# A planned attention and dense kernel: head, zero matmuls, last transposes, halved late values and a new order

## The chip, the cores and the metric

The kernel runs on one core of a Trainium2 chip. The metric is device time in microseconds, the median of a few runs. Beside the runs there is one profiled execution with a trace; all durations below are from it.

## What is computed

Two blocks, A and B, are applied twice, with the same weights both times.

```python
x = x + A(layernorm(x)); x = x + B(layernorm(x))
x = x + A(layernorm(x)); x = x + B(layernorm(x))

# A: 64 segments of 32 rows, one after the other
for s in range(64):
    h = concat([mem, xs])              # 8 memory rows + 32 rows = 40
    q, k, v = h @ Wq, h @ Wk, h @ Wv   # 512 -> 32 heads x 128
    p = softmax(where(mask, q @ k.T * scale, -1e9))
    o = (p @ v) @ Wo                   # 40 x 512
    mem, out[s] = o[:8], o[8:]
# B: relu(x @ w1) @ w2                 # 512 -> 1376 -> 512
```

There are 2048 rows in bf16. The memory makes A a recurrence: a segment can't start its projections before the output projection of the segment before it.

## The kernel before

**Two layers side by side.** The two applications of A run interleaved in 68 steps. Step k works on segment k of the first layer and segment k-4 of the second (`DELTA` = 4). In steps 4 to 63 both are active, and each matmul streams 80 columns, 40 of each layer; in steps 0 to 3 and 64 to 67 only one is, with 40 columns. The columns of a step lie transposed in one of two tiles HT, and the weights stay in SBUF.

**One step.** `step_values` multiplies HT's columns by Wv (L1006). `queries_keys` makes q and k in units of 4 heads, 16 matmuls each into a bank of `work`. `scores` does the score matmuls (L1090), then mask, maximum and subtraction on DVE (L1101, L1105, L1108), exp on ACT (L1112), sum and reciprocal on DVE (L1115, L1118), and the multiply that gives P on DVE or POOL (L1132). P is turned by a matmul with the identity, and ACT and DVE copy it to PT (L1155, L1157). `attend` multiplies PT by the values (L1174), and ACT copies the result to OT (L927, the line of the copy helper). `project` multiplies OT by Wo into the one bank `st`, in five parts, one per unit; "project.2" is the third of them. From `st` the eight new memory rows go to the next step's HT, and the rows go to OX. All matmuls that may run whole or in two 64-column tiles go through `across` and have line L671.

**After each odd step,** `finish_pair` takes 64 rows of each layer: a DMA transpose of OX on SP (L888), the residual add on DVE (L892), then `dense_layer` with its `layernorm` (statistics L712 and L715 on DVE, eps and power on POOL L718 and L719, norm on DVE L722, a DMA transpose on SP L736), w1 (L671), relu, w2 (L798 for 64 rows), an add (L813) and the store (L913). For the very last pair nothing is left to run beside this chain.

**The start.** `load_weights` issues the weights in the order Wv, Wq, Wk, Wo from SP (the first piece) and POOL. `prepare` loads the first 128 rows of x and the memory from ACT's queue, clears tiles on DVE and POOL, and clears the five `work` banks with copies from the zeroed V0 on ACT and DVE. The first rows are normalised (`prepare_group`), turned on PE, copied to a tile by ACT, and copied from there into HT by POOL in `prep_x` (L946). While weights land, PE makes the values of groups 1 to 7 of 128 rows ahead of time and stores them. The values of groups 8 to 15 are made later by `late_values`, eight ops of four 512-column matmuls for a pair of groups, put into the odd steps at certain step numbers (`SPREAD`); some odd steps so have two of them, some one, and from step 49 on none.

**The order.** Nothing is ordered by hand. `Plan` collects all ops with modelled costs and dependences, and `order` plays them through and emits one static order per engine. Which op goes next on PE is decided by a priority, `PERIOD * step + PLACE[op, phase]`; `phase` tells apart the first steps, even and odd steps and the last ones. For other engines the priority comes from the users of an op, less an entry of `AHEAD`. `RULE` holds four numbers: how far ahead a start may be looked for, how much staying in a tile mode is worth, and two for ops marked `spare`. `PAIRED` lists which projections (queries, keys, Wo) may run in two 64-column tiles ("64-column mode") rather than whole. An op with two engines takes the one on which it ends sooner by the model.

Of the kernel before, what the change touches and what calls it, by code (L numbers as in the profile page):

```python
# [9 lines left out]
F32 = mybir.dt.float32  # L10
# [20 lines left out]
RULE = (0.077, 191.201, 3554579.029, 1242705613.066)  # L31
PERIOD = 42.8582
PLACE = {
# [153 lines left out]
}  # L187

LOAD = {("v", 0): 4.4, ("v", 1): 3.8, "o": 2.95}
REST, SLOW = 2.75, 6.0  # L190

EARLY, SPREAD = 7, (0, 0, 2, 4, 4, 6, 8, 10)

# [225 lines left out]
def kernel(  # L419
# [185 lines left out]
    def prepare():  # L605

        def zero_columns():
            for t in HTs:
                nc.vector.memset(t[:], 0.0)
# [731 lines left out]
```

## Time and profile before

| quantity | value |
|---|---|
| median of 3 runs | 1618.84 us (1618.56 to 1620.61) |
| span of the profiled execution | 1619.3 us |
| instructions in it | 94084 |
| PE work per two steps in the middle | 47.1 us |
| last weights landed | 50.6 us |
| end of the last project | 1601.79 us |

The page of the profile gives the busy time of each engine, the span in 40 slices, the DMA queues, a chain of work that ended last, and the costliest groups of instructions. Here is what the slices look like for PE, and for the DMA engines:

```profile
PE   7899999999999999999999999999999999999996
...
DMA  9721111111111111111111111111111111111000
```

A digit is the busy share in tenths of a slice of 40 us. PE is nearly full from the second slice to the last but one, and the DMA engines only while the weights load. A row such as `L671 PE MATMUL st<-OT,Wo_sb` is a group: line, engine, operation, output, inputs.

### The profile page before, as it was taken

Reading aid. Unit: us, or ns where it says so; the run is one execution under the profiler, and the core shown is the slowest. Engines: PE = TensorE matmul, PEld = TensorE weight load, DVE = VectorE, ACT = ScalarE, POOL = GpSimd, SP = SyncE. Lnnn points to the kernel's source line nnn. Section 1 sums busy time; section 2 is a strip of 40 time slices with the busy share of each in tenths; the row PEclk is TensorE's granted clock in tenths of the full one; section 3 lists DMA queues with packets and bytes.
Section 4 is the critical chain, followed back from the end, with each engine's and each line's share of the span. In section 5 each row is a group of like instructions: output and inputs, shape, how many; then the busy total and the mean of one; then the engine's idle time right before and its main releaser. Section 6 shows DMA issues by size and latency. Waiting matters only on the chain.

```text
span 1619.3 us, 94084 instructions
## 1 busy us (share of the span) xinstructions
PE 1573.6 (97%) x42673; PEld 1355.0 (84%) x42673; DVE 1050.2 (65%) x2974; ACT 1058.4 (65%) x2672; POOL 160.7 (10%) x395
## 2 busy tenths in 40 slices
PE   7899999999999999999999999999999999999996
PEld 4678888888888888888888888888888888888875
DVE  4466666766766676676667667666766766676663
ACT  5567666766666676666667666666766666676663
POOL 4210000001100000110000011000000000000000
PEclk9999999999999999999999999999999999999998
DMA  9721111111111111111111111111111111111000
GB/s 374 244 50 35 30 29 36 33 34 40 36 31 30 36 33 34 40 33 33 31 36 33 34 40 33 34 31 36 33 34 30 30 28 27 27 27 27 21 15 11
DMA packets 88065, 74.03 MB, mean 46 GB/s; under 512 B 60584, under 2 KB 74000, under 8 KB 87664
## 3 DMA queue, kind: packets, MB, share of 16 engines
q1 hardware_dynamic: 81168, 46.64, 12.9%
q0 software_dynamic: 5328, 20.32, 3.3%
q8 instruction: 334, 5.47, 1.4%
q10 hardware_dynamic: 1168, 1.06, 0.2%
q14 instruction: 67, 0.55, 0.1%
HBM read 33.50 MB, written 11.93 MB: 28 GB/s over the span
## 4 chain that ended last, share of the span: by engine, by line
PE 95%; ACT 2%; DMA 1%; POOL 1%; issue 1%; DVE 1%; POOLq 0%; SPq 0%; DVEq 0%; ACTq 0%
PE work L671 40%; PE st L671 19%; PE fill L1006 16%; PE fill L671 11%; PE work L1174 4%; PE work L1090 3%; ACT OT L927 1%; DMA xr<-OX 0%; ACT HT L927 0%; PE fill L798 0%; DMA xnM<-xr 0%; DMA V<-vw 0%; ACT es L1112 0%; POOL ln L719 0%; ACT qT L927 0%
## 5 line engine op out<-in xcount | busy, mean ns | idle before, releaser
L671 PE MATMUL work<-HT,Wk_sb 128*128 128x80 bf16 (+2 forms) x9184 | 357.3, 199 | 11.5 <-ACT HT L927 9.3
L671 PE MATMUL work<-HT,Wq_sb 128*128 128x80 bf16 (+2 forms) x10624 | 357.6, 200 | 0.0
L671 PEld LDWEIGHTS <-Wk_sb 128*128 128x128 bf16 (+1 forms) x9184 | 326.3, 101 | 32.2 <-ACT HT L927 13.7
L671 PEld LDWEIGHTS <-Wq_sb 128*128 128x128 bf16 (+1 forms) x10624 | 328.4, 104 | 29.1 <-issue 16.2
L671 PE MATMUL st<-OT,Wo_sb 128*128 128x80 bf16 (+1 forms) x8704 | 334.7, 199 | 5.4 <-ACT OT L927 3.6
L671 PEld LDWEIGHTS <-Wo_sb 128*128 128x128 bf16 x8704 | 317.7, 99 | 15.4 <-issue 10.0
L1006 PE MATMUL fill<-Wv_sb,HT 128*64 128x512 bf16 x2176 | 281.8, 383 | 0.9 <-POOL HT L946 0.5
L927 ACT CAST kT<-work 128x320 bf16<-128x320 f32 (+1 forms) x517 | 211.8, 410 | 107.5 <-PE work L671 66.3
L927 ACT CAST qT<-work 128x320 bf16<-128x320 f32 (+1 forms) x505 | 207.7, 412 | 73.7 <-PE work L671 25.7
L1101 DVE TENSOR_TENSOR es<-work,maskb 128x320 f32<-128x320 f32 (+2 forms) x340 | 134.8, 405 | 127.6 <-PE work L1090 119.9
L927 ACT CAST OT<-work 128x320 bf16<-128x320 f32 (+1 forms) x351 | 132.6, 414 | 129.2 <-PE work L1174 128.6
L1155 ACT ACTIVATE PT<-work,half 128x320 bf16<-128x320 f32 (+1 forms) x406 | 181.8, 477 | 8.7 <-DVE PT L1157 4.0
L927 ACT CAST vw<-fill 128x512 bf16<-128x512 f32 x228 | 133.9, 587 | 76.3 <-PE fill L1006 73.4
L1006 PEld LDWEIGHTS <-HT 128*64 128x64 bf16 x2176 | 101.9, 110 | 62.7 <-issue 2.3
L1112 ACT ACTIVATE es<-es 128x320 f32<-128x320 f32 (+2 forms) x340 | 134.1, 405 | 18.3 <-DVE es L1108 14.4
L1108 DVE TENSOR_TENSOR es<-es,mx 128x320 f32<-128x320 f32 (+2 forms) x340 | 135.3, 406 | 4.5
L1157 DVE TENSOR_SCALAR PT<-work,half 128x160 bf16<-128x160 f32 (+2 forms) x274 | 116.2, 445 | 31.4 <-PE work L671 29.7
L1105 DVE TENSOR_REDUCE mx<-es 128x8 f32<-128x320 f32 (+2 forms) x340 | 132.6, 398 | 4.6
L1115 DVE TENSOR_REDUCE sm<-es 128x8 f32<-128x320 f32 (+2 forms) x340 | 129.7, 390 | 2.7 <-ACT es L1112 2.3
L1132 DVE TENSOR_TENSOR P<-es,sm 128x320 bf16<-128x320 f32 (+2 forms) x307 | 127.8, 426 | 5.4
L892 DVE TENSOR_TENSOR xg<-xg,xr 128x512 f32<-128x512 f32 (+1 forms) x34 | 23.5, 692 | 161.1 <-DMA xr<-OX 160.9
L1090 PEld LDWEIGHTS <-qT 128*40 128x40 bf16 x4096 | 87.4, 98 | 34.6 <-ACT qT L927 0.3
(91 smaller groups left out, 1701.1 us busy)
## 6 DMA issues: line engine op xcount, KB each, us to landing
V<-vw SPq DMA_DIRECT2D x240, 48.0 KB
V<-vh SPq DMA_DIRECT2D x120, 64.0 KB
Wq_sb<-in_A_Wq_dram POOLq DMA_DIRECT2D x2, 2048.0 KB, 20.3
Wk_sb<-in_A_Wk_dram POOLq DMA_DIRECT2D x2, 2048.0 KB, 24.8
Wo_sb<-in_A_Wo_dram POOLq DMA_DIRECT2D x2, 2048.0 KB, 36.4
vh<-vg SPq DMA_DIRECT2D x32, 128.0 KB
Wv_sb<-in_A_Wv_dram POOLq DMA_DIRECT2D x1, 2048.0 KB, 11.2
vh<-w_sb POOLq DMA_DIRECT2D x4, 512.0 KB, 7.7
```

The costliest lines, as they stand in the source:

```text
L671: nc.tensor.matmul(out_[u:v, :], lhsT=lhsT[:, u:v], rhs=rhs, start=start, stop=stop, tile_position=(0, u), **more)
L927: nc.scalar.copy(out=out_, in_=in_)
L1006: nc.tensor.matmul(vp[64 * b:64 * b + 64, :], lhsT=cols(c4), rhs=Wv_sb[:, c4, n * 512:(n + 1) * 512], start=(c4 == 0), stop=(c4 == NC4 - 1 ...
L1090: nc.tensor.matmul(v[64 * g2:64 * g2 + L, a, i, b, :], lhsT=qT[:, hi, a * L:(a + 1) * L], rhs=kT[:, hi, a * L:(a + 1) * L], start=True, st ...
L1101: nc.vector.tensor_tensor(out=flat(es[:, A]), in0=flat(sp[:, A]), op=ALU.add, in1=maskb[:, a_lo:a_hi, :].unsqueeze(2).to_broadcast([128, n ...
L1105: nc.vector.tensor_reduce(out=mx[:, As], in_=es3(), axis=AX.X, op=ALU.max)
L1108: nc.vector.tensor_tensor(out=es3(), in0=es3(), op=ALU.subtract, in1=mx[:, As].unsqueeze(2).to_broadcast([128, ns * na, L]))
L1112: nc.scalar.activation(out=es[:, A], in_=es[:, A], func=ACTF.Exp, scale=SCALE)
L1115: nc.vector.tensor_reduce(out=sm[:, As], in_=es3(), axis=AX.X, op=ALU.add)
L1132: (nc.gpsimd if eng == POOL else nc.vector).tensor_tensor(out=o, in0=flat(es[:, A]), op=ALU.mult, in1=sm[:, As].rearrange("p (a s) -> p a ...
L1155: nc.scalar.activation(out=o, in_=i, func=ACTF.Copy, scale=half[:, b:b + 1])
L1157: nc.vector.tensor_scalar_mul(out=o, in0=i, scalar1=half[:, b:b + 1])
```

## The change

It has six parts.

1. **First rows.** The load of x rows 0 to 127 moves from ACT's queue to SP, ahead of the first piece of Wv; in the plan that piece waits for the issue.
2. **Zero matmuls.** A new 128x256 tile `none` is zeroed by DVE. `spin` multiplies it by itself into a bank, two matmuls of 256 columns. Five of these clear the `work` banks in place of five copies from V0; eight more (`WARM`) only run. The first queries and keys wait for the clearing of their banks.
3. **A shorter first layernorm.** For the first rows and the last pair, eps is added on DVE, the power stays on POOL. For the first rows an added copy (`first`) puts the turned rows straight into HT, and `prep_x(0)` goes.
4. **The last pair** turns OX on PE (`turn_near`, four matmuls of 128 columns in a 64-column tile) instead of by DMA, followed by 20 zero matmuls (`idle(2.2)`). Its second transpose is on PE too, with a copy (`keep_near`).
5. **Late values** are planned as two ops of two matmuls in place of one of four.
6. **The order** is planned anew: all numbers in `RULE`, `PERIOD`, `PLACE`, `PAIRED` and `AHEAD` are others. The program has 44797 matmuls in place of 42673; 46 are zero matmuls, the rest come from ops that are now in 64-column mode (two matmuls for one). 270 queries and keys ops are in that mode, before 150. 28 more of the multiplies L1132 are on POOL.

The diff, its tables cut to a line each:

```diff
-RULE = (0.077, 191.201, 3554579.029, 1242705613.066)
-PERIOD = 42.8582
+RULE = (0.0787279, 46.129, 9.15314e+07, 211.005)
+PERIOD = 11.86222
...
+WARM = 8
...
-                    t, o = min((c for c in starts if c[0] <= due and c[0] + room * c[1].cost[e] * c[1].spare <= due), key=rank)
+                    t, o = min((c for c in starts if c[0] <= due and c[0] + room * c[1].cost[e] * c[1].spare <= due), key=rank,
+                               default=(t, o))
...
+    def get_x():
+        nc.sync.dma_start(out=xb0[:, :], in_=A_x[0, 0:128, :])
+
     def load_weights():
 
+        plan.op(SP, 0.78, get_x, w=[xb0, "x0"], lag=0.0)
...
+        def zero_none():
+            nc.vector.memset(none[:], 0.0)
...
-        def get_x():
-            nc.scalar.dma_start(out=xb0[:, :], in_=A_x[0, 0:128, :])
...
-            def zero_bank(eng, t=t):
-                copy_on(eng, t[:], V0[:].rearrange("p q n -> p (q n)").bitcast(F32)[:, 0:512])
+            def zero_bank(t=t):
+                spin(t)
...
+    def spin(bank):
+
+        for u in range(2):
+            nc.tensor.matmul(bank[:, 256 * u:256 * u + 256], lhsT=none[:, 0:128], rhs=none[:, :], start=True, stop=True)
+
+    def idle(t, r=()):
+        bank, n = b_fill.buf(), max(1, int(t / 0.218))
+
+        def spins():
+            for _ in range(n):
+                spin(bank)
+
+        plan.op(PE, t, spins, r=["none", *r], w=[bank], count=2 * n)
...
+        early, quick = not isinstance(xnT, Buf), near or xnT is first_rows
...
         def power():
-            nc.gpsimd.tensor_scalar_add(out=ln[R, 7:8], in0=ln[R, 7:8], scalar1=LN_EPS)
+            (nc.vector if quick else nc.gpsimd).tensor_scalar_add(out=ln[R, 7:8], in0=ln[R, 7:8], scalar1=LN_EPS)
+            if not quick:
+                raise_()
+
+        def raise_():
             nc.gpsimd.tensor_tensor(out=ln[R, 7:8], in0=ln[R, 7:8], in1=mhalf[R, :], op=ALU.pow)
...
+        if near:
+            plan.op(PE, 0.01 + 1.72e-3 * n, turn, r=[xn, "ident"], w=[tp], tile=EITHER, count=4)
+            copy_op(NC4 * n, keep_near, r=[tp], w=[xnT])
+            return xnT
...
+        if xnT is first_rows:
+            copy_op(NC4 * SEG, first, r=[tp], w=htx(0, 0))
...
+        last = j == NP + D2 - 1
+        if last:
+            y = b_fill.buf()
+
+        def turn_near():
+            for c4 in range(NC4):
+                nc.tensor.matmul(y[PR:2 * PR, 128 * c4:128 * c4 + 128], lhsT=ox[:, c4, PR:2 * PR], rhs=ident[:, :],
+                                 start=True, stop=True, tile_position=(0, PR))
...
-        plan.op(SP, XBAR[0] + XBAR[1] * NC4, turn, r=[ox], w=[y], lag=XBAR[2])
+        if last:
+            plan.op(PE, 0.22, turn_near, r=[ox, "ident"], w=[y, "turned"], tile=COL64, count=NC4)
+            idle(2.2, ["turned"])
+        else:
+            plan.op(SP, XBAR[0] + XBAR[1] * NC4, turn, r=[ox], w=[y], lag=XBAR[2])
...
-        plan.op(PE, 0.2165 * NC4, mm, r=[*on(pair[0]), *on(pair[1]), *gate], w=[vp], tile=EITHER, spare=True,
-                count=NC4)
+        for c0 in range(0, NC4, 2):
+            def mm(cols, c0=c0):
+                for c4 in (c0, c0 + 1):
...
+            plan.op(PE, 0.433, mm, r=[*on(pair[0]), *on(pair[1]), *gate], w=[vp], tile=EITHER, spare=True, count=2)
...
-    plan.mark(0, "s")
-    prep_x(0)
```

More of the change, by code (lines that the diff above doesn't have):

```diff
@@ new lines @@
+    ("*layernorm.aggr", 1): 54551538274992652288, ("*layernorm.first", 1): -15140200627925014,
+    ("*layernorm.keep", 1): -349948822785553596416, ("*layernorm.norm", 1): -15140200627913234,
+    ("*layernorm.power", 1): 350004080033075429376, ("*layernorm.raise_", 1): 262488285178343948288,
+    ("*layernorm.stats", 1): -906.966, ("*prepare_group.load", 1): -54520433886651039744,
+    ("*values.ev", 1): 10798138046876852224, ("attend.ev", 0): -6284291257622319104, ("attend.ev", 1): 1079.491,
@@ new lines @@
+    ("attend.ev", 2): -2553479593618.246, ("bulk.land", 1): -238860144121.9,
+    ("dense_layer.relu", 0): -14914902342738771968, ("dense_layer.relu", 1): 10.441,
+    ("dense_layer.relu", 2): -135955653579501.906, ("dense_layer.relu_last", 0): 8630611085116452864,
+    ("dense_layer.relu_last", 1): 94558522.384, ("dense_layer.relu_last", 2): -135955653582153.484,
+    ("early_stores.put", 1): -2338178960349301760, ("finish_pair.add", 0): -754598561880401024,
+    ("finish_pair.add", 1): -541211854841342208, ("finish_pair.add", 2): -5135522821684.899,
@@ new lines @@
+    ("finish_pair.add0", 0): -8449851934466816, ("finish_pair.add0", 1): -2116007360007716096,
+    ("finish_pair.add1", 0): 678562308116700160, ("finish_pair.add1", 2): 517137148556446.5,
+    ("finish_pair.store", 0): -2736302177266691072, ("finish_pair.store", 2): -554122428120319,
+    ("finish_pair.turn", 0): 771228859628232576, ("finish_pair.turn", 1): -8411911657729126400,
+    ("finish_pair.turn", 2): 855769499775299712, ("finish_pair.widen", 0): -3434171858064559616,
+    ("finish_pair.widen", 1): -11285277819407153152, ("get_x", 1): -10804293557987115008,
@@ new lines @@
+    ("late_values.ev", 0): -338731664576501841920, ("late_values.put", 0): 124.155,
+    ("layernorm.aggr", 0): -338774959185562828800, ("layernorm.aggr", 1): -1283017268359357952,
+    ("layernorm.aggr", 2): -2124137526600.683, ("layernorm.keep", 0): -86307786047708640,
+    ("layernorm.keep_near", 2): -1932750949110.553, ("layernorm.norm", 0): -8180445813364675,
+    ("layernorm.norm", 1): 1256955092211969.5, ("layernorm.norm", 2): -587212723712585.5,
+    ("layernorm.power", 0): -3425991412251194880, ("layernorm.power", 1): 8667933725116555264,
@@ new lines @@
+    ("layernorm.power", 2): -179841382886347776, ("layernorm.raise_", 2): 180391610330498048,
+    ("layernorm.stats", 0): -513018287628265216, ("layernorm.stats", 1): -558147728977931648,
+    ("layernorm.stats", 2): -620728644676.763, ("layernorm.turn_far", 0): 1118984946535674880,
+    ("layernorm.turn_far", 1): 2119073176186372864, ("layernorm.turn_far", 2): -513925009903168.938,
+    ("load_dense.dma1", 1): -2518505793790285312, ("load_dense.dma2", 1): -537535825433483264,
+    ("load_group.get", 0): 1068285834928873088, ("load_group.get", 1): -352507446103958159360,
@@ new lines @@
+    ("load_group.load", 0): 674877631977439232, ("load_group.load", 1): 309263599505791320064,
+    ("load_weights.dma", 1): 174994470155083907072, ("make_ident", 1): 524983410226391613440,
+    ("make_mask", 1): 487564700809337831424, ("place_values.dma", 0): -2736302177266692608,
+    ("place_values.dma", 1): -6024653512617976, ("prep_x.cp", 0): -2948860633222666752,
+    ("prep_x.cp", 1): 349988940071307706368, ("prep_x.cp", 2): 179804397606783520,
+    ("prepare.get_memory", 1): 9013136272599680, ("prepare.keep", 1): 271359371850913447936,
@@ new lines @@
+    ("prepare.make_half", 1): 10785635464923846656, ("prepare.place", 1): -14327787264.792,
+    ("prepare.zero", 1): 111823167.023, ("prepare.zero_columns.zero", 1): -10793200354345601024,
+    ("prepare.zero_none", 1): 111823008.502, ("prepare.zero_ox", 1): 251674778347272568832,
+    ("prepare_group.load", 0): -503980667476090368, ("prepare_group.put", 0): -392362853562742272,
+    ("prepare_group.put", 1): -2338178004908725248, ("project.ev", 0): -109848075148066832,
+    ("project.ev", 1): -341038992002229338112, ("project.ev", 2): -1035549021077084.875,
@@ new lines @@
+    ("project.first", 1): -161879.785, ("project.rows", 0): -342058079058195644416,
+    ("project.rows", 1): -10204126385068992, ("project.rows", 2): 516497770743318.875,
+    ("queries_keys.ev", 0): -2688.654, ("queries_keys.ev", 1): 3379306714640166,
+    ("queries_keys.ev", 2): -1932750948659.773, ("scores.block", 0): -13588549336362629120,
+    ("scores.block", 1): 3.988, ("scores.block", 2): 1288500730644.738, ("scores.exp", 0): 13647408900884832256,
+    ("scores.exp", 1): -18932611.033, ("scores.exp", 2): -630011255086.4,
@@ new lines @@
+    ("scores.keep", 0): -340848835228960686080, ("scores.keep", 1): 3379306714647110.5,
+    ("scores.keep", 2): -1932750948086.011, ("scores.mul", 0): 179804397606588544,
+    ("scores.mul", 1): 2468249049887821.5, ("scores.mul", 2): 50246.546, ("scores.recip", 0): -14.277,
+    ("scores.recip", 1): 1068.112, ("scores.recip", 2): -1288500730305.69, ("scores.sub", 0): -13647408900884832256,
+    ("scores.sub", 1): 18932637.161, ("scores.sub", 2): -658489475543.995, ("scores.top", 0): -8271002289903067136,
@@ L187 @@
+    ("scores.top", 1): -70.887, ("scores.top", 2): -1923468696638.604, ("scores.total", 0): 8271002289903065088,
+    ("scores.total", 1): -48.963, ("scores.total", 2): 1288500731007.345, ("values.ev", 0): -2690.806,
+    ("values.ev", 1): 3379306714642456, ("values.ev", 2): -1932750949652.126,
 }
@@ L512, in dma @@
                     q.dma_start(out=W_s[c][:, :, cs], in_=W_v[c][:, :, cs])
-            bulk(POOL if (c, p0) != ("v", 0) else SP, 0.78, dma, (c, p0), n, w=[("W", c, p0 + i) for i in range(n)],
+            bulk(POOL if (c, p0) != ("v", 0) else SP, 0.78, dma, (c, p0), n, w=[("W", c, p0 + i) for i in range(n)], r=["x0"] if (c, p0) == ("v", 0) else [],
                  rate=LOAD.get((c, p0), LOAD.get(c, REST)))
@@ L588 @@
     V0 = sb("V0", [128, 4, 512])
+    none = sb("none", [128, 256])
     OT = sb("OT", [128, H, 2 * L])
@@ L605, in prepare, with zero_columns, zero @@
     def prepare():
-        def zero_columns():
-            for t in HTs:
-                nc.vector.memset(t[:], 0.0)
+        def zero_none():
+            nc.vector.memset(none[:], 0.0)
+        def zero_columns(i):
+            def zero():
+                nc.vector.memset(HTs[i][:], 0.0)
+            plan.op(DVE, 0.2, zero, w=[("HTm", i), *[("HTx", i, a, c) for a, c in ((0, 0), (1, X1))]])
         def make_half():
@@ L635, in place @@
             nc.vector.tensor_copy(out=HTs[0][:, :, MO[0]:MO[0] + M], in_=mem0T[:])
-        columns = [("HTm", i) for i in range(2)] + [("HTx", i, a, c) for i in range(2) for a, c in ((0, 0), (1, X1))]
-        plan.op(ACT, 0.45, get_x, w=[xb0, "x0"])
-        plan.op(ACT, 0.45, get_memory, r=["x0"], w=[mb0, "start"])
-        plan.available("memory", 7.5)
-        plan.op(DVE, 0.4, zero_columns, w=columns)
+        plan.op(ACT, 0.45, get_memory, w=[mb0, "start"])
+        plan.available("memory", 5.5)
+        plan.op(DVE, 0.13, zero_none, w=["none"])
+        for i in range(2):
+            zero_columns(i)
         plan.op(DVE, 0.25, make_half, w=["half"])
@@ L656, in prepare @@
         for i, t in enumerate(b_work.tiles):
-            def zero_bank(eng, t=t):
-                copy_on(eng, t[:], V0[:].rearrange("p q n -> p (q n)").bitcast(F32)[:, 0:512])
-            copy_op(512, zero_bank, r=[("V0", 0, 0)], w=[("bank", i)])
-        plan.op(POOL, 0.6, make_ident, r=[("issued", "v", 1)], w=["ident"])
+            def zero_bank(t=t):
+                spin(t)
+            plan.op(PE, 0.43, zero_bank, r=["none"], w=[("bank", i)], count=2)
+        for i in range(WARM):
+            idle(0.43 if i < 3 else 0.22, [("bank", j) for j in range(5)])
+        plan.op(POOL, 0.6, make_ident, w=["ident"])
         plan.op(POOL, 2.3, make_mask, w=["mask"])
@@ L694 @@
     hold, stores = [None], []
+    first_rows = p_xn[0].buf()
     def on(t):
@@ L702, in halves_of, with layernorm @@
         return t[:, :, :].rearrange("p q (h t) -> p q h t", h=2)
-    def layernorm(x, rows, xnT, lo=0, n=128, to=None, halved=False):
-        ln, xn, tp = p_ln.buf(), p_xr.buf(), b_fill.buf() if halved else None
+    def layernorm(x, rows, xnT, lo=0, n=128, to=None, halved=False, near=False):
+        ln, xn, tp = p_ln.buf(), p_xr.buf(), b_fill.buf() if halved or near else None
         R = slice(lo, lo + n)
         to = lo if to is None else to
-        early = not isinstance(xnT, Buf)
+        early, quick = not isinstance(xnT, Buf), near or xnT is first_rows
         def stats():
@@ L733, in keep, with keep_near, first @@
                     i.rearrange("p (q c h s) -> p q c h s", q=NC4, h=2, s=HS))
+        def keep_near(eng):
+            copy_on(eng, xnT[:, :, to:to + n], tp[:, 0:NC4 * n].rearrange("p (c t) -> p c t", c=NC4))
+        def first(eng):
+            copy_on(eng, HTs[0][:, :, 0:SEG].rearrange("p q (h s) -> p q h s", h=2),
+                    tp[:, 0:NC4 * n].rearrange("p (q h c s) -> p q h c s", q=NC4, h=2, s=HS)[:, :, :, 0, :])
         def turn_far():
@@ L741, in layernorm @@
         plan.op(DVE, 0.11 + pd, aggr, w=[ln])
-        plan.op(POOL, 0.80, power, r=["half"], w=[ln])
+        if quick:
+            plan.op(DVE, 0.09, power, w=[ln])
+            plan.op(POOL, 0.40, raise_, r=["half"], w=[ln])
+        else:
+            plan.op(POOL, 0.80, power, r=["half"], w=[ln])
         plan.op(DVE, 0.453 + pd, norm, r=[x, ln, *rows], w=[xn])
+        if near:
+            plan.op(PE, 0.01 + 1.72e-3 * n, turn, r=[xn, "ident"], w=[tp], tile=EITHER, count=4)
+            copy_op(NC4 * n, keep_near, r=[tp], w=[xnT])
+            return xnT
         if not halved:
@@ L747, in layernorm, with dense_layer @@
         plan.op(PE, 0.01 + 1.72e-3 * n, turn, r=[xn, "ident"], w=[tp], tile=EITHER, count=4)
+        if xnT is first_rows:
+            copy_op(NC4 * SEG, first, r=[tp], w=htx(0, 0))
         copy_op(NC4 * n, keep, r=[tp, *([xnT.buf] if early else [])], w=[xnT.key if early else xnT])
         return xnT
-    def dense_layer(x, rows, act):
+    def dense_layer(x, rows, act, near=False):
         lo, n = PR * act[0], PR * len(act)
-        xnT = layernorm(x, rows, p_xm.buf(), lo, n)
+        xnT = layernorm(x, rows, p_xm.buf(), lo, n, near=near)
         hT = p_h.buf()
@@ L826, in prepare_group @@
             xb = xb_tiles[0]
-            plan.available(xb0, 4.5)
+            plan.available(xb0, 3.9)
         else:
@@ L837, in prepare_group @@
                     w=[xb, *(rows if g == 1 else [])], lag=SLOW if early else 2.45)
-        xnT = layernorm(xb, rows, p_xn[0].buf() if g == 0 else Early(g) if early else Late(g, first), halved=True)
+        xnT = layernorm(xb, rows, first_rows if g == 0 else Early(g) if early else Late(g, first), halved=True)
         if g == 0:
@@ L892, in add @@
             nc.vector.tensor_tensor(out=x[R, :], in0=x[R, :], in1=y[R, :], op=ALU.add)
-        plan.op(SP, XBAR[0] + XBAR[1] * NC4, turn, r=[ox], w=[y], lag=XBAR[2])
+        if last:
+            plan.op(PE, 0.22, turn_near, r=[ox, "ident"], w=[y, "turned"], tile=COL64, count=NC4)
+            idle(2.2, ["turned"])
+        else:
+            plan.op(SP, XBAR[0] + XBAR[1] * NC4, turn, r=[ox], w=[y], lag=XBAR[2])
         plan.op(DVE, t_dve(512) + PART[DVE] * (len(act) < 2), add, r=[y, x], w=[("x", j, a) for a in act])
-        yp, total, t_total = dense_layer(x, halves(j), act)
+        yp, total, t_total = dense_layer(x, halves(j), act, last)
         if 0 in act:
@@ L977, in late_values @@
         xl = pair[0].buf
-        def mm(cols):
-            for c4 in range(NC4):
-                across(cols, vp[:, :], xl[:, c4, 0, :, :].rearrange("p g t -> p (g t)"),
-                       Wv_sb[:, c4, n * 512:(n + 1) * 512], start=(c4 == 0), stop=(c4 == NC4 - 1))
         def ev(eng):
             copy_on(eng, vg[:, q, :], vp[:, :])
-        plan.op(PE, 0.2165 * NC4, mm, r=[*on(pair[0]), *on(pair[1]), *gate], w=[vp], tile=EITHER, spare=True,
-                count=NC4)
+        for c0 in range(0, NC4, 2):
+            def mm(cols, c0=c0):
+                for c4 in (c0, c0 + 1):
+                    across(cols, vp[:, :], xl[:, c4, 0, :, :].rearrange("p g t -> p (g t)"),
+                           Wv_sb[:, c4, n * 512:(n + 1) * 512], start=(c4 == 0), stop=(c4 == NC4 - 1))
+            plan.op(PE, 0.433, mm, r=[*on(pair[0]), *on(pair[1]), *gate], w=[vp], tile=EITHER, spare=True, count=2)
         copy_op(512, ev, r=[vp], w=[("vg", q)])
@@ L1063, in queries_keys @@
             plan.op(PE, 16 * t_mm(n), mm,
-                    r=[("HTm", i), *[d for a in range(a_lo, a_hi) for d in htx(i, a)], ("W", nm, p)], w=[qp, dst],
+                    r=[*([("bank", b) for b in range(5)] if k == 0 else []), ("HTm", i), *[d for a in range(a_lo, a_hi) for d in htx(i, a)], ("W", nm, p)], w=[qp, dst],
                     tile=SOFT if a_hi - a_lo == 2 else WHOLE, count=16)
```

37 lines of the change are left out of this document (removed), and 235 rows, old and new, of tables (PAIRED, PLACE).

## The prediction

> **What bounds it now.** The page's first part first, then the waits of PE, then windows by stage.
>
> ```profile
> PE 1573.6 (97%) x42673; PEld 1355.0 (84%) x42673; DVE 1050.2 (65%) x2974; ACT 1058.4 (65%) x2672; POOL 160.7 (10%) x395
> ```
>
> PE is busy 97% of the span. So only its waits, its cold clock or its work can yield time. Spacing PE's matmuls as they step when nothing holds them (n/2.4 + 2.5 ns for n columns, at least 25, half of it in a 64-column tile; it gives the 36 ns that 80 columns take in the timeline), all 42673 take 1540.6 us. The other 78.7 us of the 1619.3 us span are loss, and I place them by stretch: 11.5 before 12.16 us; 3.3 in 12 to 20; 11.4 in 20 to 160; 34.9 over steps 4 to 63 together (a little of it inside 160); 3.6 in steps 64 to 67; 17.5 after the last project.
>
> ```profile
> PE work L671 <- ACT HT L927: 9.3, 31, 0.3
> PE fill L671 <- DMA xnM<-xr: 8.4, 1, 8.4
> PE st L671 <- ACT OT L927: 3.6, 21, 0.3
> ```
>
> A row is who waits for whom: us, times, longest. The largest single wait is at the end; the other two come once in two steps. Three stretches bear on the change (start:end, length, busy PE, PEld, DVE, ACT, POOL, clock, DMA share, GB/s):
>
> ```profile
> 0.00:12.16 12.16, 1.46 (x13) 0.94 (x13) 7.49 (x23) 3.93 (x6) 10.95 (x28) 1.00 0.85 318
> ...
> 17.76:50.60 32.84, 30.52 (x584) 20.91 (x582) 14.78 (x54) 21.05 (x53) 7.58 (x17) 1.00 1.03 384
> 50.60:115.20 64.60, 59.55 (x1698) 47.86 (x1695) 35.07 (x136) 37.33 (x120) 11.37 (x25) 1.00 0.39 122
> ...
> 1601.80:1615.30 13.50, 5.10 (x66) 4.26 (x65) 2.36 (x6) 1.31 (x4) 0.79 (x2) 0.62 0.08 16
> ```
>
> Until 50.6 us the DMA is full; the last rows of Wo land at 50.61. The last stretch ran mostly at half clock (0.62). The clock of 1.00 in the first row misleads: until 17.76 us pairs of 512-column matmuls step at 0.426 us, after it at 0.214.
>
> **Head.** Before, x is there at about 3.0 us, but the statistics start at 5.10, after DVE has zeroed V0 and two banks. Then eps on POOL at 7.16, pow 7.50 (0.57), norm 8.10, turn 8.64 (0.61), ACT copy 9.28 (0.59), and a POOL copy that waits behind weight issues:
>
> ```profile
> 11.80 0.30 POOL L946 COPY HT<-xnA 128x128 bf16<-128x128 bf16 x1
> 12.16 3.62 PE L1006 MATMUL fill<-Wv_sb,HT 128*64 128x512 bf16 x16 [0.47 <-POOL HT L946]
> 18.39 1.03 PE L1006 MATMUL fill<-Wv_sb,HT 128*64 128x512 bf16 x8
> ```
>
> After: banks are zeroed by PE, eps is on DVE, the ACT copy writes HT0 itself. In the new order POOL's pow stands behind memory-mask work and ends at about 8.6 by the durations of these rows, so norm 9.0, turn 9.5, copy to 10.4: values start 1.8 us earlier (bounds 0.9 to 2.3). The 26 zero matmuls of 256 columns stand ahead of it on PE, behind one DVE memset: they start near 3.9 us, step at 0.218 while cold, and end near 8.1, so the memory turn queued behind them comes 1.6 us later than before (6.46), still ahead of the norm. Clock windows of 3.41 us fit the rises and falls of this trace; 4.11 to 7.52 would be the first full one, so the values run at full clock: the cold loss in 12 to 20 was 2.76 us. Another 3 us or so comes from smaller waits.
>
> But not all of it reaches the end. On SP the x issue (0.48 us) now precedes Wv's first piece, which so starts that much later, its landing at 6.12 still 4 us early; on ACT memory goes 0.42 us sooner. The other weights land where they did: the DMA share is 1.03. Project.2 of step 0 needs Wo of 50.61; before it started at 55.10, after PE would be ready at 46.5 to 47.5 and must wait. So at most 4.5 us come from here. From there to step 4's first queries PE has 53.3 us of paced work (before 52.2 plus 7.9 of loss, 115.2). With a loss of 5.5 to 6, mostly the two stalls of instruction fetch at 49.9 (1.40) and 62.85 (1.85) and the waits on OT, step 4 starts at 109.5 to 110: **gain 5.2** (2 to 7).
>
> **Steps 4 to 63.** Two steps take 47.1 us where the pace says 45.86. Even steps lose 0.12, odd ones 0.68 with two late values, 1.00 with one (11 steps), 1.55 with none (8, steps 49 to 63). Of an odd step 0.44 to 0.47 is the wait for HT (11.8 in all), 0.11 the OT wait before project.4, 0.31 that before project.2 (20 steps, 6.2), the rest waits for P.
>
> ```profile
> 773.46 1.31 PE L671 MATMUL st<-OT,Wo_sb 128*128 128x80 bf16 x32 [0.15 <-ACT OT L927]
> 776.46 0.93 PE L671 MATMUL work<-HT,Wk_sb 128*128 128x80 bf16 x21 [0.30 <-ACT HT L927]
> ```
>
> The new order puts the second half of a late value (0.43 us) ahead of project.2, which covers 0.3 us in the 11 one-late steps: 3.3. HT and project.4 keep their waits, since the same op still precedes them. POOL takes 28 more multiplies L1132, now 128x320 wide; before it had only
>
> ```profile
> L1132 POOL TENSOR_TENSOR P<-es,sm 128x160 bf16<-128x160 f32 x32 | 14.5, 454 | 165.9 <-DVE sm L1118 165.0 <-PE work L1090 1.0
> ```
>
> 454 ns at 160, 320 at 80: between 0.72 (same slope) and 0.91 (twice) at 320, against 0.43 on DVE. I take 0.75; the no-late steps then keep their 0.4 us wait for P. The gaps in the other steps shift by tenths either way: **gain 4** (-5 to +6).
>
> Paired tiles: 270 instead of 150 queries/keys ops run in two 64-column tiles. The rows show 0.573 us for such an op either way, a pair in 36 ns as one whole matmul; five mode switches fewer at 0.1. Cost 0. The Trainium skill's page "TensorEngine Tiling (Array Packing)", section "Gotcha 2: Feature Incompatibilities", says column tiling excludes the fast weight load; if that bound here, each pair would take two slots, 120 x 16 x 36 ns = 69 us more by an estimate, but in the trace it takes one, so under 1 in 100.
>
> **Steps 64 to 67.** attend.4 now stands where project.3 waited 0.47 for OT, twice, and P's waits shrink: 1.8. The w2 part of pair 65's dense (1.41) moves behind the last project, into the shadow of the tail's chain: with the switches **2.0 + 1.8 = 3.8** (2 to 4.5).
>
> **Tail.** The chain of waits (start, length):
>
> ```profile
> 1602.10 2.42 DMA xr<-OX
> 1604.54 0.70 DVE xg L892
> 1605.26 0.70 DVE ln L712
> ...
> 1606.25 0.22 POOL ln L718
> 1606.51 0.62 POOLq L1336
> 1607.16 0.56 DVE xr L722
> 1607.77 2.31 DMA xnM<-xr
> 1610.12 2.61 PE fill L671 x44
> 1612.73 2.51 PE fill L798 x19
> ```
>
> After, from the last project: ACT copy 0.3, turn on PE 0.2, DVE add and statistics 1.4; pair 65's two adds (0.85) may stand between statistics and aggregation; eps and pow 0.9, norm 0.56, turn at +4.85, copy, dense at +5.55. The two transposes' 4.73 become some 1.2. At full clock w1 takes 1.28 (44 x 29 ns) instead of 2.61 and w2 1.2 (11 pairs of 256 columns at 0.109) instead of 2.51, so PE ends at +8.35 where it was +13.6: **gain 5.2**. The 20 zero matmuls (2.2) follow the turn on PE and run beside the adds; the next turn, queued behind them, is ready later than they end (+3.1). If they weren't there, the clock falls and 3.3 of it go.
>
> **Sum.** 5.2 + 4 + 3.8 + 5.2 = 18.2: 1619.3 becomes 1601.1. The span lies 0.5 above the median of 1618.84, so the median run should be **1601** (1600.6 rounded up, as waits I can't see rather add). About 0.2% (3.2 us) is what a measurement tells from no change.
>
> **Rivals.**
> Clock low in the tail (0.11): zero matmuls don't hold it. Last matmul 1601.8, drop at 1604.96, rise at 1615.20, all on a grid of 3.41 us on which a window busy 7% counted as idle and one busy half did not raise it. After, the longest gap is about 1.75 us. If it still falls: turn, w1 and w2 at half, +3.3, and up to 1 in the head: 1605. The Trainium skill, "TensorE: Matmul & The Clock Gate", Part 1, wants an idle window of 3.4 us for a drop; by that the forecast stands, and the drop of before agrees.
>
> New waits in odd steps (0.14): POOL at 0.91 or DVE's new order holds P or HT 0.3 us longer in each of 30 pairs, +9: 1610. For it: POOL's multiply is twice DVE's. Against: DVE is busy 65%.
>
> Slower (0.07): instruction fetch becomes the bound. One packet is 128 matmuls:
>
> ```profile
> q8 instruction: 334, 5.47, 1.4%
> ```
>
> 5.47 MB in 334 packets, 16 KB each; 42673 matmuls over 334 are 128. PE stalled twice 1.4 us after such a landing. Pairs in 64-column tiles eat packets twice as fast: 80 blocks of 128 are shorter than 3.6 us after, 27 before. With a floor of F us per block the added stall is 6.8 us at 3.2, 14.2 at 3.4, 23.7 at 3.6. It decides from F = 3.5: +19 cancels the gain, at 3.6 the time is 1624. Against: blocks of 2.86 us ran free at 130 us, and over 192 matmuls the new minimum is that of before (4.40 against 4.33).
>
> Forecast 0.67 (1594 to 1604); the rest of 0.01 is mishap. All but the fetch and a part of the second rival end below 1615.6: faster 0.90, same 0.04, slower 0.06. The range 1594 to 1610 takes in forecast, clock and the milder half of the new waits; below 1594 only if HT's wait went too.
>
> **What would show it.** Right: values near 10.4 us; pairs stepping at 0.214 there; step 4 near 110; no PE wait for DMA xnM; clock 1.0 after the last project and 8 to 9 us from there to PE's end; the waits on HT as before. Wrong: a step 4 above 113; odd steps over 1.3 us above pace; rows "PE work <- issue" in runs of 64-column tiles (fetch); 0.62 again in the tail.

## The result, and the profile after

The changed kernel takes 1614.11 us in the median of five runs, the kernel before 1620.61 in five runs beside it: a ratio of 0.9967 with a 95% interval of 0.9955 to 0.998. That is 0.33% faster, 5 to 7 us, where 18 were forecast. The profiled execution has a span of 1613.6 us, 5.7 less than before.

The page, busy time and the queue that fetches instructions:

```profile
PE 1577.2 (98%) x44797; PEld 1364.6 (85%) x44797; DVE 1002.2 (62%) x2916; ACT 1059.3 (66%) x2702; POOL 173.2 (11%) x420
...
q8 instruction: 350, 5.73, 1.6%
```

The waits of PE (us, times, longest):

```profile
PE work L726 <- ACT HT L1017: 8.7, 29, 0.3
...
PE work L726 <- issue: 4.0, 5, 1.2
PE fill L1096 <- issue: 3.9, 5, 1.0
PE work L1264 <- DMA V<-vw: 2.2, 4, 0.8
...
PE st L726 <- ACT OT L1017: 0.5, 2, 0.3
```

The big wait for DMA xnM is gone, and that for OT ahead of project fell from 3.6 to 0.5 us. The wait for HT stayed, as forecast. New are eleven waits with "issue", which nothing in the profile releases, ten of them in these two rows; before had two (1.9 and 1.4). And there are waits for V, which a DMA fills from vw.

To cut the spans at the same places, I take the copies of the memory rows to HT at the end of steps 3 and 63 (ACT, `HT<-st`):

| stretch | before | changed | gain | forecast |
|---|---|---|---|---|
| to the end of step 3 | 114.42 | 112.07 | 2.4 | 5.2 |
| steps 4 to 63 | 1415.1 | 1420.4 | -5.3 | +4 |
| from there to the end | 89.7 | 81.2 | 8.6 | 9.0 |

So the end came as forecast, the head gave half, and the middle lost where it was to gain. The tail by its timeline (start, length):

```profile
1602.67 2.34 PE L711 MATMUL fill<-none 128*128 128x256 bf16 x20
...
1605.77 0.29 PE L726 MATMUL fill<-ident,xr 128*128 128x64 bf16 x4 [0.76 <-DVE xr L782]
...
1606.52 1.67 PE L726 MATMUL fill<-xnM,w_sb 128*128 128x64 bf16 x44 [0.46 <-ACT xnM L1017]
...
1608.12 1.39 PE L875 MATMUL fill<-w_sb,hT 128*64 128x256 bf16 x22
```

From the last project's end at 1601.1 the turn comes after 4.7 us (forecast 4.85), w1 after 5.4 (5.55), PE's end after 8.4 (8.35); w1 and w2 run at full clock.

In the middle, this is what an "issue" wait looks like. The timeline of PE around the first in the steady part:

```profile
285.32 1.32 PE L726 MATMUL work<-HT,Wq_sb 128*64 128x80 bf16 x64
286.47 1.32 PE L726 MATMUL work<-HT,Wk_sb 128*64 128x80 bf16 x64
287.62 0.60 PE L1096 MATMUL fill<-Wv_sb,HT 128*64 128x512 bf16 x4
288.76 0.59 PE L1096 MATMUL fill<-Wv_sb,HT 128*64 128x512 bf16 x3 [0.55 <-issue]
```

PE runs 128 matmuls in 64-column tiles in 2.3 us, then stops in the middle of a run of equal matmuls whose inputs are all there. The next stops are at 383.12, 477.70, 572.71 and 667.40, then 1189.82 and 1284.37 us: mostly 94.5 us apart, which is four steps.

### The profile page after: what moved, and what is told of

Its sections match the earlier page's. It is cut to its first block, busy times and chain, and to the rows that moved or that the text cites. A ratio compares the mean times of both kernels' runs of the same rounds, so it can differ in the third digit from the quotient of the medians.

```text
span 1613.6 us, 98246 instructions
## 1 busy us (share of the span) xinstructions
PE 1577.2 (98%) x44797; PEld 1364.6 (85%) x44797; DVE 1002.2 (62%) x2916; ACT 1059.3 (66%) x2702; POOL 173.2 (11%) x420
## 4 chain that ended last, share of the span: by engine, by line
PE 91%; issue 3%; DMA 2%; DVE 2%; ACT 2%; POOL 0%; SPq 0%; POOLq 0%; DVEq 0%; ACTq 0%
PE work L726 38%; PE st L726 18%; PE fill L1096 15%; PE fill L726 11%; PE work L1264 4%; PE work L1180 3%; DMA V<-vw 1%; DMA hT<-in_A_x_dram 1%; ACT HT L1017 0%; DVE ln L768 0%; ACT vw L1017 0%; DMA xr<-OX 0%; PE fill L875 0%; DMA xe<-in_A_x_dram 0%; ACT OT L1017 0%
## 5 line engine op out<-in xcount | busy, mean ns | idle before, releaser
L726 PEld LDWEIGHTS <-Wo_sb 128*128 128x128 bf16 (+1 forms) x8736 | 320.9, 99 | 22.7 <-issue 2.9
L726 PE MATMUL st<-OT,Wo_sb 128*128 128x80 bf16 (+2 forms) x8736 | 337.7, 199 | 1.3 <-ACT OT L1017 0.5
L1191 DVE TENSOR_TENSOR es<-work,maskb 128x160 f32<-128x160 f32 (+2 forms) x340 | 129.9, 400 | 148.7 <-PE work L1180 146.1
L1017 ACT CAST vw<-fill 128x512 bf16<-128x512 f32 x259 | 151.8, 586 | 83.1 <-PE fill L1096 76.8
L1245 ACT ACTIVATE PT<-work,half 128x320 bf16<-128x320 f32 (+2 forms) x412 | 182.2, 467 | 30.9 <-PE work L726 15.9
L1202 ACT ACTIVATE es<-es 128x160 f32<-128x160 f32 (+2 forms) x340 | 133.6, 407 | 4.7 <-DVE es L1198 3.6
L1205 DVE TENSOR_REDUCE sm<-es 128x4 f32<-128x160 f32 (+2 forms) x340 | 131.5, 398 | 4.9 <-ACT es L1202 2.1
L1198 DVE TENSOR_TENSOR es<-es,mx 128x160 f32<-128x160 f32 (+2 forms) x340 | 130.6, 403 | 2.4
L1247 DVE TENSOR_SCALAR PT<-work,half 128x320 bf16<-128x320 f32 (+2 forms) x268 | 121.4, 461 | 12.3 <-PE work L726 11.4
L1195 DVE TENSOR_REDUCE mx<-es 128x4 f32<-128x160 f32 (+2 forms) x340 | 127.8, 395 | 1.6
L1264 PE MATMUL work<-PT,V 128*64 128x80 bf16 (+1 forms) x1536 | 108.5, 202 | 3.8 <-DMA V<-vw 2.2
```

Of the source, the lines that this page charges most:

```text
L726: nc.tensor.matmul(out_[u:v, :], lhsT=lhsT[:, u:v], rhs=rhs, start=start, stop=stop, tile_position=(0, u), **more)
L1017: nc.scalar.copy(out=out_, in_=in_)
L1191: nc.vector.tensor_tensor(out=flat(es[:, A]), in0=flat(sp[:, A]), op=ALU.add, in1=maskb[:, a_lo:a_hi, :].unsqueeze(2).to_broadcast([128, n ...
L1195: nc.vector.tensor_reduce(out=mx[:, As], in_=es3(), axis=AX.X, op=ALU.max)
L1198: nc.vector.tensor_tensor(out=es3(), in0=es3(), op=ALU.subtract, in1=mx[:, As].unsqueeze(2).to_broadcast([128, ns * na, L]))
L1202: nc.scalar.activation(out=es[:, A], in_=es[:, A], func=ACTF.Exp, scale=SCALE)
```

## What the stops are: two theories

**Theory 1: instruction packets.** Queue q8 brings PE's instructions in packets of 16 KB. Each matmul comes with a weight load, so 44797 matmuls in 350 packets are 128 to a packet. I counted the instructions of PE in program order and divided by 256. All nine stops of over half a microsecond after the change, and the two of before, stand at the same fraction of a packet, 0.76, and each ends 1.2 to 1.6 us after a packet of q8 has landed. The packet is asked for about when PE enters the packet before it (0.9 us early to 0.9 late for most), and the transfer mostly takes 0.9 to 1.4 us. So PE has only one packet ahead, and a packet that it uses up in less than some 3.1 us can be followed by a stop. From one steady stop to the next, four steps on, lie 5376 instructions, just 21 packets: the packet ends come back to the same ops. By the pace of the matmuls, the seven packets ahead of the steady stops last 2.18 to 2.65 us. Nearly all matmuls of the one shown above, which lasts 2.65 us, are in 64-column tiles.

**Theory 2: the new order.** PE waits for engines or DMAs that the new order makes late, such as POOL's multiplies or V's transfer, and the stops with "issue" belong to the ops at which they stand.

## Experiments

**Packet ends moved.** The zero matmuls of the head are cut:

```diff
-        for u in range(2):
-            nc.tensor.matmul(bank[:, 256 * u:256 * u + 256], lhsT=none[:, 0:128], rhs=none[:, :], start=True, stop=True)
+        w = 512 // cuts[0]
+        for u in range(cuts[0]):
+            nc.tensor.matmul(bank[:, w * u:w * u + w], lhsT=none[:, 0:128], rhs=none[:, 0:w], start=True, stop=True)
```

`cuts[0]` is 8 in the head and 2 in the tail.

> The 26 zero matmuls of 256 columns in the head are cut into 104 of 64 columns: the same time on PE, the same order, but 78 more matmuls, so that all instructions of PE behind them lie 0.61 of a 16 KB packet later. Theory 1 (instruction packets: PE stops at a packet's end when the 128 matmuls in it ran in under about 3.2 us): the stops of the changed kernel at 288.8, 383.1, 477.7, 572.7, 667.4, 1189.8 and 1284.4 us go, and new ones of 0.4 to 1.3 us stand near 145, 240, 335, 429, 524, 619, 857, 952, 1046, 1141, 1236, 1331 and 1425 us, one in each four steps; span 1613.6 + 3 = 1616 to 1618. Theory 2 (the stops belong to the new order of the ops, which wait for other engines or a DMA): they stay at the same ops and the time stays within 1 us, 1612 to 1615.

The timeline of PE, its stops:

```profile
144.91 0.41 PE L1100 MATMUL fill<-Wv_sb,HT 128*64 128x512 bf16 x2 [0.98 <-issue]
...
239.84 0.23 PE L730 MATMUL work<-HT,Wk_sb 128*64 128x80 bf16 x2 [0.61 <-issue]
...
429.41 0.27 PE L730 MATMUL work<-HT,Wk_sb 128*64 128x80 bf16 x5 [0.66 <-issue]
...
1045.10 0.27 PE L730 MATMUL work<-HT,Wk_sb 128*64 128x80 bf16 x5 [0.80 <-issue]
...
1329.83 0.27 PE L730 MATMUL work<-HT,Wk_sb 128*64 128x80 bf16 x5 [0.85 <-issue]
```

All seven old stops are gone. New ones stand at 11 of the 13 places named, each within 2 us; at 524 and 619 there is none. Theory 2 can't explain that, since the ops and their order are the same. The time did not rise as theory 1 had it: 1616.04 us, ratio 0.9971 (0.9959 to 0.9982), which can't be told from the change's 0.9967. Steps 4 to 63 take 1420.5 us in place of 1420.4: more stops, but shorter ones (0.25 to 0.98 us).

**Other modes, same order.** For the order of the changed kernel, a search picked the mode of each op that may run both ways, with the fewest mode switches for which packets are paced at 3.5 us or more (two of 334 stay under 3.4); the result stands in the kernel as a list of 195 ops.

```diff
-        for o in plan.order():
+        for o in other(plan.order()):
...
+    def other(ops):
+        for n, o in enumerate([o for o in ops if o.eng == PE]):
+            if n in OTHER:
+                o.mode = WHOLE if o.mode == COL64 else COL64
+        return ops
```

> The order of all ops of the changed kernel is kept; 195 of the PE ops that may run whole or in two 64-column tiles are emitted in the other mode (184 of them whole), chosen so that no stretch of 128 matmuls between two packet ends is paced under 3.4 us; 42790 matmuls in place of 44797, 313 mode switches as before. Theory 1: no wait with 'issue' above 0.4 us in the steps from 4 on, 7 to 8 us less there and 2 to 3 less in the head: span 1603 to 1606, median run about 1605. Theory 2: whole and paired ops take the same 0.573 us, so nothing changes: 1612 to 1615.

The median is 1603.18 us (ratio 0.9895, 0.988 to 0.991), 11 us under the change, with a span of 1601.8. Its page (91 of the 42790 matmul records are missing from this trace), and its waits of PE from 115 to 1535 us, which are all that the view lists there:

```profile
PE 1567.3 (98%) x42699; PEld 1361.5 (85%) x42790; DVE 1001.7 (63%) x2916; ACT 1058.0 (66%) x2702; POOL 172.5 (11%) x420
```

```profile
PE work L740 <- ACT HT L1031: 8.4, 28, 0.3
PE work L1278 <- DMA V<-vw: 1.6, 5, 0.7
PE st L740 <- ACT OT L1031: 0.8, 5, 0.2
```

No "issue" is left there. Steps 4 to 63 take 1411.1 us, 9.3 less than in the change and 4.0 less than before: just the gain that was forecast for the order.

Where the 9.3 us come from tells more than their sum. Most of the ops whose mode was changed stand in even steps, and these take as long as in the change (medians 24.89 and 24.90). The gain lies in the odd steps (22.60 and 22.03), whose queries, keys and output projections kept their modes. Step 27 has the same 660 matmuls in the same modes in both kernels: it takes 23.12 us in the change, with the stop of 1.10 us at 667.40, and 21.82 here. So an op's mode as such costs no time. But each change of mode moves the packet ends behind it, and where these fall among the paired queries and keys of an odd step decides whether PE stops. Of the 9.3 us, 6.4 lie in the eight odd steps in which the change has an "issue" wait; the rest is not traced to stops.

To the end of step 3 it takes 109.46 us, 5.0 less than before (forecast 5.2), and from step 63 to the end 81.2. Taken together that is 17.5 us of the 18.2. This kernel beats both.

**All paired, in the kernel before.** To see the floor by itself:

```diff
+        for o in ops:
+            if o.eng == PE and o.soft:
+                o.mode = COL64
```

> The kernel before, its order of ops kept; all queries, keys and output projections that work on both layers are emitted in two 64-column tiles: 63313 matmuls in place of 42673, 506 mode switches in place of 318, paced sum 1559.4 in place of 1540.6. Theory 1 (one packet of 128 matmuls can't be had in less than some 3.1 us): 138 us are missing to that floor where before it was 2, so the span is 1619 + 19 + 90 to 136 (a part lies in waits that are there anyway) = 1730 to 1775, with hundreds of waits with 'issue'. Theory 2 (paired ops cost nothing of themselves, and the stops of the changed kernel were a matter of its order): 1619 + 19 = 1638.

The span is 1911.8 us, in a single run. The waits of PE and the queue:

```profile
PE work L671 <- issue: 151.2, 170, 1.8
PE st L671 <- issue: 31.8, 56, 1.5
PE work L1090 <- issue: 18.1, 24, 1.3
```

```profile
q8 instruction: 495, 8.11, 1.8%
```

The direction is theory 1's, but my floor was too low: 1912 - 1619 - 19 = 274 us are stops. Summing what each packet lacks to a floor, 3.1 us gives 138 and 3.5 gives 259. One packet that is used up too fast meets a floor of about 3.1; many in a row meet one of 3.5 or slightly more, the requests then being mostly 3.3 to 3.9 us apart.

**The same search on the kernel before**, with a list of 49 ops in place of the 195:

> The kernel before, its order kept, with the modes of 49 ops chosen by the same packet rule (42880 matmuls, 317 switches). Theory 1: before had only its two stops at 49.9 (1.40 us) and 62.8 (1.85), so at most 3 us are to be had, 1616 to 1619; the rest of what the run with other modes gains over the kernel before is the change's own. If choosing modes is a gain whatever the order: 1605 to 1612.

It takes 1617.26 us, ratio 0.9985 (0.9976 to 0.9994), 2.7 us less. The two stops did not go; they shrank to 1.00 and 1.23 us. So choosing modes is worth little where few packets starve; the rest of the 17 us is the change's own.

**Multiplies on DVE.**

```diff
-                o.fn(o.eng)
+                o.fn(DVE if o.kind == "scores.mul" else o.eng)
```

> All multiplies that give P run on DVE, at their places in the order; nothing else is changed. Theory 1 (the odd steps lose to instruction packets): within 1.5 us of the changed kernel, 1612 to 1616. Theory 2 (POOL's multiplies of 128x320, which take longer than DVE's 0.43 us, hold P and with it PE): 0.3 us in up to 28 steps are given back, 1606 to 1610.

It takes 1621.5 us, ratio 1.0019 (1.0006 to 1.0031): 7 us more than the change, which neither theory had. Even steps take 25.13 us in place of 24.89 (medians), which makes up the 7 us. The multiply now stands on DVE ahead of a copy of PT, for which attend waits after the w1 matmuls. Step 34, first in the change, then in this run:

```profile
838.81 0.54 DVE L1247 TENSOR_SCALAR PT<-work,half 128x320 bf16<-128x320 f32 x1
...
839.48 0.20 PE L1264 MATMUL work<-PT,V 128*64 128x80 bf16 x2
```

```profile
841.93 0.32 DVE L1222 TENSOR_TENSOR P<-es,sm 128x160 bf16<-128x160 f32 x1
...
842.17 0.55 DVE L1247 TENSOR_SCALAR PT<-work,half 128x320 bf16<-128x320 f32 x1
...
842.76 0.23 PE L1264 MATMUL work<-PT,V 128*64 128x80 bf16 x2
```

In the even steps attend starts 0.05 us after that copy ends and mostly 0.24 to 0.26 us after the last matmul of w1, where in the change it mostly follows after 0.03. The view lists no wait there, as the matmuls before are still shown as running. So POOL's multiplies pay, though each is slow: they keep DVE free for the copies. In the changed kernel, by form:

```profile
L1222 POOL TENSOR_TENSOR P<-es,sm 128x320 bf16<-128x320 f32 x30 | 21.7, 724 | 222.4 <-PE work L726 109.0 <-DVE sm L1208 77.0 <-ACT PT L1245 36.5
```

724 ns is the lower end of my 720 to 910.

**Late values in one piece**, at the place of the first half, on top of the other modes:

```diff
+        if o.kind == "late_values.mm" and name in firsts:
+            first, fn = firsts.pop(name), o.fn
+            first.fn = lambda cols, a=first.fn, b=fn: (a(cols), b(cols))
+            first.count = 4
+            continue
```

> As the run with other modes (1603.2), but the two halves of each late value are emitted together, at the place of the first, and the modes are chosen anew for the same packet rule (42790 matmuls, 313 switches). If the second half covered the wait of project.2 for OT as forecast: 0.3 us comes back in each step that has that wait, 11 to 32 of them: 1606 to 1612. If other work covers it in the new order: within 1 us of 1603.

It takes 1609.55 us, ratio 0.9936 (0.9924 to 0.9949), 6.4 more; 6.2 of it lie in steps 4 to 63. The halving is worth about twice the 3.3 that I gave it. The waits there (115 to 1535 us):

```profile
PE work L1294 <- ACT PT L1275: 2.7, 4, 0.7
PE st L756 <- ACT OT L1047: 1.5, 10, 0.2
```

The second half covers not only OT ahead of project.2 but also a wait of attend for PT.

**No zero matmuls in the tail:**

```diff
+            if o.kind == "idle.spins" and o.step > 0:
+                continue
```

> The 20 zero matmuls behind the last turn are left out. If they hold the clock: the gap on PE from 1602.6 to 1605.8 becomes 3.2 us long, the clock is at half for w1 and w2 of the last pair, and the span grows by up to 3 us (1616.5). If the short gap alone is enough: the clock stays, 1613 to 1614.

The tail's timeline:

```profile
1608.03 0.39 PE L726 MATMUL fill<-ident,xr 128*128 128x64 bf16 x4 [3.12 <-DVE xr L782]
1608.88 2.61 PE L726 MATMUL fill<-xnM,w_sb 128*128 128x64 bf16 x44 [0.46 <-ACT xnM L1017]
1611.43 2.56 PE L875 MATMUL fill<-w_sb,hT 128*64 128x256 bf16 x22
```

The clock fell at 1607.83: w1 takes 2.61 us instead of 1.67 and w2 2.56 instead of 1.39, and the way from the last memory rows to the end is 30.6 us in place of 28.3. So here the zero matmuls are worth 2.3 us. The median, 1616.18 us (ratio 0.9977, 0.9967 to 0.9986), shows 1 to 2 with overlapping intervals.

**Short zero matmuls in the head**, on top of the other modes:

```diff
-                spin(bank)
+                if t < 1:
+                    for u in range(2):
+                        nc.tensor.matmul(bank[:, 8 * u:8 * u + 8], lhsT=none[:, 0:128], rhs=none[:, 0:8], start=True, stop=True)
+                else:
+                    spin(bank)
```

> As the run with other modes (1603.2), but the 16 zero matmuls of the head that only run stream 8 columns each in place of 256; those that clear banks stay. Their busy time on PE falls by about 2 us. If they set the clock: it stays at half until the values fill a window, some 2.5 us of PE work more ahead of 50 us; as PE then waits for the last weights with 1 us to spare, 1 to 2 us of it reach the end: 1604 to 1605. If the other zero matmuls suffice, or the weights hide it: 1602.5 to 1603.5.

1604.2 us, ratio 0.9901 (0.9885 to 0.9916), against 0.9895: the runs can't tell the two apart. The clock did rise later, at 18.91 us in place of 7.12. The profiled execution, the slowest of the four at 1606.89, also has a stop of 2.97 us at 63.82 and half clock for one window after it.

**A wider floor**, with a list of 210 ops:

> The changed kernel's order with the modes of 210 ops chosen for a wider floor: 3.6 us for a packet, and 4.3 for the first 19, while the weights fill the DMA queues (42788 matmuls, 313 switches). The run with other modes still had stops of 0.50, 0.55 and 0.33 us there. If they are packets too: 1602 to 1603, up to 1.4 us under it; if not, 1603 to 1604.

1605.09 us, ratio 0.9905 (0.989 to 0.992): no gain. In the head stops remain at packet ends, of 1.16 us at 83.1 for one, although PE takes over 4 us for each packet there. The request itself goes out late, up to 4 us after PE entered the packet before. Why is open.

## Why the prediction was wrong

**The step that failed** is the price of the paired tiles, "Cost 0", with the rival on instruction fetch that was to guard it (0.07). Its rows were right: an op takes 0.573 us both ways. But it takes twice the instructions, and where such ops fill a packet, PE uses it up before the next is there. The price was 9.3 us in steps 4 to 63, which came back with other modes in the same order. So the rival came true in part, at about half the 19 us from which it was to decide. Its own line had 6.8 us at a floor of 3.2 and 14.2 at 3.4; none of that went into the sum. I weighed it down by "blocks of 2.86 us ran free at 130 us" and by stretches of 192 matmuls. The first was a packet that lasted 2.85 us while the transfer of the next took only 0.98; the second is no unit that the fetch knows. Cut at the packets' real ends, the changed kernel has ten packets paced at 2.66 us or less in steps 4 to 63, the kernel before none. The seven steady stops follow seven of the ten; after the other three the view shows no "issue".

The paced sum of 1540.6 us, from which the prediction reckons the losses, holds 0.1 us for each of the 318 mode switches, which its sentence does not say; in the trace of before a switch takes 0.08 to 0.20 us.

**Steady gain of 4:** 4.0, once the stops are taken away. That it fits so well is in part luck. The halves cover 6, not 3.3, and POOL's multiplies gain where I feared a loss. Waits for V (2.2 us, with other modes 1.6, before 0.4) take some of it back; I had not looked at them. And one profile is not the next: with short zero matmuls, which have the same modes, steps 4 to 63 take 1408.4 us, a gain of 6.7.

**Head 5.2:** 2.4 in the profile. Values start at 11.03 us, not 10.4. PE turns the memory behind 22 zero matmuls at half clock, at 8.86; DVE copies it ahead of the norm, which so starts at 9.46. And the table load of ACT, which the bank copies used to trigger at 2.24 us, waits for DVE and then stands in the way:

```profile
8.86 0.26 PE L666 MATMUL fill<-ident,ob 8*128 8x8 bf16 x4
...
9.16 0.17 DVE L670 COPY mem0T<-fill 128x32 bf16<-128x32 bf16 x1 [2.80 <-PE fill L666]
...
9.42 1.28 ACT L1017 ACT_TABLE_LOAD   x1 [9.42 <-DVE ln L771]
...
10.71 0.27 ACT L1017 CAST HT<-fill 128x128 bf16<-128x128 f32 x1
10.88 0.59 ACT L1017 CAST xnA<-fill 128x512 bf16<-128x512 f32 x1
11.03 0.57 PEld L1096 LDWEIGHTS <-HT 128*64 128x64 bf16 x8 [0.85 <-ACT HT L1017]
```

The prediction let the clock rise at 7.52, by the windows in the trace of before. But the windows lie elsewhere in each execution: in this trace it rose at 9.88, with other modes at 7.12, where values start at 10.30.

After a stop of 1.22 us at 83.84 the clock was at half for one window (start:end, length, busy PE, PEld, DVE, ACT, POOL, clock, DMA share, GB/s):

```profile
81.57:84.98 3.41, 2.19 (x87) 2.01 (x83) 1.49 (x7) 1.70 (x6) 0.64 (x2) 1.00 0.37 117
84.98:88.39 3.41, 3.41 (x64) 2.40 (x62) 2.65 (x13) 1.88 (x8) 0.00 (x0) 0.50 0.33 103
```

That costs half the window, 1.7 us. In three of the five runs, those of 1612.97 to 1614.11 us, the mean clock is 1.000, in the other two 0.999 and 0.998. With other modes the head gave 5.0, and in the profile with the multiplies on DVE, whose values start at 11.04 and whose clock holds, 5.1. So of the 2.8 us missing in the head the fall of the clock makes 1.7, and the late start of the values need not reach the end of step 3.

**Steps 64 to 67 and tail, 9.0:** 8.6, and both parts came as forecast (3.6 and 5.0). The zero matmuls hold the clock, as said; without them it falls.

**The Trainium skill's rule** that column tiling excludes the fast weight load ("TensorEngine Tiling (Array Packing)", "Gotcha 2: Feature Incompatibilities") shows no price here: even steps, in which most of the 184 ops stand that were made whole again, take 24.89 us in the change and 24.90 with these ops whole (medians).

## What to carry to other kernels

An engine that is 97% busy with short instructions can be bound by their fetch: count the instructions between packet ends, and compare the time they take with request, transfer and start (here some 3.1 us for 128 matmuls). Twice the matmuls for the same work can cost time, even at the same pace, where they fill a whole packet. Where the order is fixed, choosing which ops are cut in two against the real packet ends took 11 us off without moving an op.

## What the runs showed of the hardware that I had not expected

The clock can drop after a far shorter pause than I took from the tail of before: the window ahead of the drop at 84.98 was busy for 2.19 of 3.41 us, while a window of before with its stop of 1.40 us, busy for less, led to no drop:

```profile
48.48:51.89 3.41, 2.01 (x30) 1.31 (x31) 1.37 (x4) 0.93 (x3) 0.00 (x0) 1.00 1.03 404
```

In the profile without the zero matmuls of the tail, whose head is the same, it fell three times before 90 us, after windows busy for 2.03, 1.82 and 2.18 us. The Trainium skill, "TensorE: Matmul & The Clock Gate", Part 1, asks for an idle window; a drop after one that was 64% busy does not fit that. What decides is open.
